# One order of a scheduled single-core kernel against another: W1 behind the inverse shuffles, k and v ahead of the filter, a last row stored in two parts

## Chip, cores and metric

The kernel runs on one core of a Trainium2 chip. The metric is the device time of one execution in microseconds (us). TensorE is called PE below, VectorE DVE, ScalarE ACT, GpSimdE POOL and SyncE SP.

## What is computed

The input x has 2048 positions and 448 channels. A long-convolution mixer comes first, then a perceptron over the positions (it multiplies along the 2048 positions, not along the channels). Cut to what matters:

```python
k_shift = sum(k_pad[:, t:t+S, :] * shift_k[:, ks-1-t] for t in range(4))   # short filter, 4 taps
kv = k_shift * v
y  = irfft(rfft(kv, padded to 2S) * rfft(ssm_k, padded to 2S))[:S]         # long convolution
h  = x + layernorm(x) * (y + kv * ssm_D)
n  = layernorm(layernorm(h))                                              # the outer and the block's own
u  = gelu(einsum("bsd,sf->bdf", n, w1) + b1)                              # w1: 2048 x 1792
h2 = h + transpose(einsum("bdf,fs->bds", u, w2) + b2)                     # w2: 1792 x 2048
```

All tensors are bfloat16. The Fourier transforms are done as matmuls with tables of sines and cosines that the kernel makes itself.

## The kernel before

Position s = 16 q + r lies in partition q, row r. So the tensors k, v and x have 16 rows of 448 channels in each of 128 partitions. The steps:

- **tables** (`emit_tables`): POOL and DVE make integer phases, ACT turns them into sines (`E`, in two halves; the second call is for the small tables `FW`, `MA`, `MB`, `MN`). A call of gelu on one column (L851) stands at the end. The functions of ACT need tables of their own; a change from Sin to gelu and back loads tables.
- **loads** (`emit_loads`), all on SP's queue: the long filter `KN` in four chunks of 112 channels, then the taps, k (`KH`) and v (`V`) in four groups of rows each, then D, b1, b2.
- **kT**: the filter is transposed on PE (L989) and copied to SBUF (`evac`, L712 on ACT and L715 on DVE). **kv**: k is transposed (L934), the short filter is done as matmuls with diagonal matrices (L953, 112 of them), and DVE multiplies with v (L959).
- **k1** and **u1** (`emit_stage1`): first stage of the transform of the filter and of kv, 128 matmuls each (L1009), copied to SBUF (L1019; L1017 adds D) and shuffled across partitions by DMAs from POOL and SP (L1025).
- **k2** and **u2** (`emit_stage2`): second stage, 64 matmuls each (L1044), copied with a scale for k (L713 on ACT, L716 on DVE) or without (L712, L715).
- **i1** (`emit_products_i1`): 16 products of the two transforms on DVE (L1077), first inverse stage on PE (L1089), copies, and the inverse shuffle by DMAs (L1113, the last ones L1102).
- **ct**: 32 transposes of `E` (L1058), whose result the next step needs. **q**: statistics of x on DVE and POOL (L1145, L1147, L1150, L1153).
- **i2** (`emit_i2`): second inverse stage (L1180, two matmuls per row), gate (L1187 ACT, L1189 DVE), combination with x (L1194) and both normalisations, which give `Q` (L1235).
- **mlp** (`emit_mlp`): first layer in 14 blocks of 128 columns over 16 rows, 112 matmuls with the first half of W1 (L1280) and 112 with the second (L1290), gelu on ACT (L1270), second layer with 14 matmuls per row (L1300), sum on DVE (L1304), stores from SP (L1308, L1311).

Matmuls whose result nobody reads (L979 "dummy", L1123 "warm") fill waits of PE.

The order on each engine is not that of the code. Every operation is recorded with what it reads and writes, and a list scheduler (`_Sched`) puts it on its engine: among the operations that are ready by its estimates, it takes the one with the smallest number in `WHEN`, a table with a rank per step. A fixed choice of ACT or DVE for the copies is in `WHERE`. Each engine then runs its own list strictly in that order and waits on semaphores. So a change of any estimate, rank or dependency can reorder all engines.

The weights come by SP's queue: the first two of four pieces of W1's first half (`W1A`) behind the u shuffles, the rest, the second half (`W1B`) and W2 behind the last inverse shuffle:

```python
op(WQ, lambda e, W, rs=rs: e.dma_start(W1A[:, rs, :], w1d[:, rs, 0:896]),
   w=[(o_W1A + 4 * h * 1792, 4 * 1792)], dmab=128 * 4 * 1792,
   after=shuf["u"] if h < 2 else [shuf["zpool"]])
```

Of the kernel before, what the change touches and what calls it, by code (L numbers as in the profile page):

```python
# [12 lines left out]
    "dummy": (104,),  # L13
    "tables": (10, 52, 67, 51, 209, 91, 219, 174,),
    "loads": (12, 63, 112, 113, 178, 199, 198, 217, 170, 184, 169, 207, 237, 226, 100,),
    "kv": (129, 6, 83, 4, 3, 157, 151, 194, 204, 85, 176, 65, 230, 9, 76, 163, 185,),
    "kT": (36, 46, 0, 53, 202, 195, 92, 71,),
    "k1": (14, 19, 30, 105, 94, 96, 116, 143, 108, 153, 127, 171, 167, 188, 190, 228,),
    "k2": (29, 28, 5, 11, 16, 27, 54, 88, 81, 57, 109, 138, 168, 172, 187, 192,),
    "u1": (8, 13, 34, 189, 24, 146, 149, 220, 175, 208, 215, 236, 48, 201, 213, 218,),  # L20
    "xload": (196, 135, 18, 31,),
    "ct": (239,),
    "bias": (43,),
    "q": (145, 130, 245, 253, 249, 242, 216, 251, 117,),
    "u2": (90, 25, 1, 26, 103, 107, 101, 99, 40, 102, 79, 15, 156, 134, 211, 214,),
    "i1": (123, 17, 106, 110, 7, 72, 55, 74, 89, 59, 177, 154, 73, 181, 222, 234,),
    "w1a": (66, 69, 98, 212,),
    "w1b": (97,),
    "warm": (224, 197, 200, 45, 39, 38, 42, 41, 162, 240, 238, 233, 227, 225, 193, 186, 124, 122, 161, 160, 158, 152,
        23, 78, 221, 56, 191, 144, 121, 95, 77, 210, 166, 86,),  # L30
    "i2": (141, 22, 35, 64, 87, 155, 147, 114, 126, 241, 75, 111, 115, 247, 203, 61, 229, 140, 179, 60, 142, 119, 137,
        139, 120, 136, 148, 128, 33, 93, 32,),
    "w2": (254,),
    "mlp": (159, 131, 248, 252, 250, 246, 244, 125, 132, 133, 37, 164, 58, 47, 50, 62, 182, 49, 118, 2, 165, 68, 44,
        150, 232, 205, 20, 231, 183, 180, 235, 173, 21, 80, 84, 206, 223, 82, 70, 243,),
}
WHERE = {
    "kv": "faffaaad",
    "kT": "ffaaafdf",
    "k1": "ffffaaadfddf",  # L40
    "k2": "fdffaddaffadffda",
    "u1": "ffafaadddddfdfad",
    "ct": "faaa",
    "bias": "a",
    "u2": "fdaafffaaaaddaaa",
    "i1": "aaffadafafaaaaaa",
    "i2": "faffdafaadaadddf",
# [518 lines left out]
def _build(nc, A_q, A_k, A_v, A_shift_k, A_ssm_k, A_ssm_D, B_w1, B_b1, B_w2, B_b2, out):  # L566
# [54 lines left out]
    with ctx:  # L621
# [65 lines left out]
        def Pb(b, i=0):  # L687
            return PS[:, b.slots[i], 0:D]
# [32 lines left out]
        def emit_tables():  # L721
# [85 lines left out]
            for h in range(2):  # L807
                sch.t0 = T_TH if h else -40.0
                o_ph = (o_pi, o_TK)[h]
                ph = view(o_ph, [64, 2, 16], i32)  # L810
                op("dve", lambda e, W, h=h, ph=ph: e.tensor_tensor(
                    out=ph[:, :, 1].rearrange("p (r x) f -> p r x f", x=8),
                    in0=frow.rearrange("p (x f) -> p x f", x=8).unsqueeze(1).broadcast_to([128, 8, 8, 16]),
                    in1=srow[:, 8 * h:8 * h + 8].unsqueeze(2).unsqueeze(3).broadcast_to([128, 8, 8, 16]), op=ALU.mult),
                   r=[(o_fr, 512), (o_s, 64)], w=[(o_ph, 8192)], n=HALF, kind="1x")
                op("dve", lambda e, W, ph=ph: e.tensor_scalar(
                    out=ph[:, :, 0], in0=ph[:, :, 1], scalar1=2048, scalar2=None, op0=ALU.add),
                   r=[(o_ph, 8192)], w=[(o_ph, 8192)], n=HALF, est=1020.0)
                phf = view(o_ph, [2 * HALF], i32)
                op("dve", lambda e, W, phf=phf: e.tensor_scalar(  # L820
                    out=phf, in0=phf, scalar1=8191, scalar2=None, op0=ALU.bitwise_and),
                   r=[(o_ph, 8192)], w=[(o_ph, 8192)], n=2 * HALF)
                op("act", lambda e, W, h=h, phf=phf: e.activation(
                    out=E[:, 16 * h:16 * h + 16, :].rearrange("p a f -> p (a f)"), in_=phf,
# [20 lines left out]
            for k, (dst, i) in enumerate(((FW, 0), (MA, 1), (MB, 1))):  # L845
# [5 lines left out]
            op("act", lambda e, W: e.activation(out=JK[:, 0:1], in_=bias[:, 1:2], func=ACT.Gelu_apprx_tanh),  # L851
               r=[(o_b + 4, 4), (o_sv, 4 * NB)], w=[(o_JK, 4)], est=1500.0)
# [7 lines left out]
        def emit_loads():  # L860
            Dq = "sp"
            for i, c in enumerate((3, 0, 1, 2)):
                sch.t0 = -20.0 + i
                op(Dq, lambda e, W, c=c: e.dma_start(KN[0:112, c, :], A_ssm_k[112 * c:112 * c + 112, :]),
                   w=[(o_KN + 4096 * c, 4096)], dmab=112 * 4096)
# [3 lines left out]
            for i, (src, c) in enumerate((("k", 3), ("k", 0), ("v", 0), ("k", 1), ("v", 1), ("k", 2), ("v", 2), ("v", 3))):  # L869
                sch.t0 = -14.0 + 0.5 * i  # L870
                if src == "k":
                    op(Dq, lambda e, W, c=c: e.dma_start(KH[:, 4 * c:4 * c + 4, :], k2d[:, 4 * c:4 * c + 4, :]),
                       w=[(o_KH + 4 * c * DB, 4 * DB)], dmab=128 * 4 * DB)
                else:
                    op(Dq, lambda e, W, c=c: e.dma_start(V[:, 4 * c:4 * c + 4, :], v2d[:, 4 * c:4 * c + 4, :]),
                       w=[(o_V + 4 * c * DB, 4 * DB)], dmab=128 * 4 * DB)
# [38 lines left out]
        def emit_kv():  # L915
# [3 lines left out]
            for i in range(2):  # L919
# [5 lines left out]
               r=[(o_ID, 256), (o_wsc, 64)], w=[(o_DG, 3584)], n=1792, kind="1x")  # L925
# [55 lines left out]

        def emit_kT():
            for i, c in enumerate((3, 0, 1, 2)):
                cw = 112
                for g in range(2):
                    sch.t0 = T_KT + 1.0 * (2 * i + g)
                    b = _Buf(psum)
                    for rr in range(8):
                        k = op("pe", lambda e, W, b=b, rr=rr, r=8 * g + rr, c=c, cw=cw: e.transpose(  # L989
                            out=Pbf(b, 0)[:, rr * cw:rr * cw + cw], in_=KN[0:cw, c, r:S:R], identity=ID[0:cw, 0:cw]),  # L990
                            r=[(o_KN + 4096 * c, 4096), (o_ID, 256)], bw=[b], kind="tr")
                    evac(lambda g=g, c=c, cw=cw: KT[:, 8 * g:8 * g + 8, 112 * c:112 * c + cw],
# [367 lines left out]
```

## Time and profile before

| what | value |
|---|---|
| median of 3 runs | 184.91 us (184.1 to 185.66) |
| the profiled execution | 185.73 us |
| its span | 183.5 us |
| PE busy | 172.5 us, 94% of the span |
| DVE busy | 108.1 us, 59% |
| ACT busy | 92.8 us, 51% |
| DMA read and written in HBM | 22.05 and 1.84 MB |

The span runs from the first to the last event that the profiler saw; the execution is 2.2 us longer. The page's second part divides the span into 40 slices of 4.6 us and gives the busy tenths of each engine. In the timelines a line has the start, the length, the engine, the source line, the operation with its shapes, how many instructions were merged, and in brackets how long the engine had stood idle and what ended that. The granted clock of PE was 1.0 throughout.

### The profile page before, as it was taken

How to read it: one execution, taken by the hardware profiler on the slowest of the kernel's cores; microseconds unless marked ns; L12 is line 12 of the kernel's file. 1: busy time of each engine (PE TensorE's matmuls, PEld its weight loads, DVE VectorE, ACT ScalarE, POOL GpSimd, SP SyncE). 2: the span in 40 equal slices, each digit the busy share in tenths (PEclk: the TensorE clock that was granted, in tenths of full speed). 3: DMA queues.
4: the chain of work that ended last, by engine and by line, in shares of the span. 5: the costliest groups of instructions: out<-in, count | busy, mean ns of one | idle time of the engine just before them, and what ended most of it. 6: DMA issues, size and time to landing. Idle time of an engine off the chain costs nothing.

```text
span 183.5 us, 3395 instructions
## 1 busy us (share of the span) xinstructions
PE 172.5 (94%) x1331; PEld 98.0 (53%) x1331; DVE 108.1 (59%) x180; ACT 92.8 (51%) x131; POOL 61.4 (33%) x155
## 2 busy tenths in 40 slices
PE   6989999999688898997999899999999999999996
PEld 2777645434233333463545355556556667777773
DVE  7978995897889999996989961000000008222221
ACT  3789877387879998966787473222102020000000
POOL 8053138299310509686788870000000000000000
DMA  6999028579849955777999999300000002011122
GB/s 176 265 377 384 12 100 326 180 261 330 303 138 379 393 207 150 221 206 237 396 405 406 424 416 425 129 0 0 0 4 0 0 0 75 4 50 50 54 96 75
DMA packets 15203, 35.11 MB, mean 191 GB/s; under 512 B 3580, under 2 KB 9244, under 8 KB 15188
## 3 DMA queue, kind: packets, MB, share of 16 engines
q1 hardware_dynamic: 12068, 28.09, 42.1%
q0 software_dynamic: 3072, 6.80, 11.4%
q8 instruction: 10, 0.16, 0.3%
q10 hardware_dynamic: 48, 0.03, 0.1%
q14 instruction: 5, 0.04, 0.1%
HBM read 22.05 MB, written 1.84 MB: 130 GB/s over the span
## 4 chain that ended last, share of the span: by engine, by line
PE 53%; DMA 14%; DVE 14%; ACT 9%; POOL 4%; SPq 3%; issue 3%; DVEq 0%; POOLq 0%
PE ps L1300 23%; PE ps L1290 12%; DMA arena<-arena 8%; PE ps L1280 6%; DMA arena<-in_A_v_dram 6%; ACT arena L712 6%; PE ps L953 4%; DVE arena L1194 3%; PE ps L1089 3%; DVE arena L1019 2%; PE ps L1009 2%; DVE arena L1077 2%; DVE arena L1145 2%; DVE arena L1235 2%; ACT arena L1019 1%
## 5 line engine op out<-in xcount | busy, mean ns | idle before, releaser
L1304 DVE SCALAR_TENSOR_TENSOR arena<-ps,arena 128x448 bf16<-128x448 f32 x16 | 10.9, 684 | 59.4 <-PE ps L1300 59.1
L1300 PE MATMUL ps<-arena 128*128 128x448 bf16 x224 | 43.9, 353 | 0.0
L1300 PEld LDWEIGHTS ps<-arena 128*128 128x128 bf16 x224 | 31.9, 144 | 11.0 <-ACT arena L1270 1.4
L1270 ACT ACTIVATE arena<-ps,arena 128x448 bf16<-128x448 f32 x14 | 8.5, 633 | 32.0 <-PE ps L1290 24.8
L1280 PE MATMUL ps<-arena 128*128 128x448 bf16 x112 | 24.2, 353 | 0.4 <-DVE arena L1235 0.4
L712 ACT CAST arena<-ps 128x896 bf16<-128x896 f32 (+1 forms) x29 | 23.4, 959 | 1.2 <-PE ps L1044 0.7
L1290 PE MATMUL ps<-arena 128*128 128x448 bf16 x112 | 23.3, 352 | 0.0
L1025 POOL DMA_DIRECT2D arena<-arena x32 | 17.6, 554 | 15.2 <-ACT arena L1019 9.3
L1019 ACT CAST arena<-ps 128x896 bf16<-128x896 f32 x17 | 14.7, 910 | 7.1 <-PE ps L1009 7.0
L1044 PE MATMUL ps<-arena 128*64 128x448 bf16 x128 | 14.9, 359 | 2.5 <-DMA arena<-arena 1.2
L712 ACT COPY arena<-ps 128x896 bf16<-128x896 bf16 (+2 forms) x14 | 13.2, 981 | 6.7 <-PE ps L989 3.5
L1280 PEld LDWEIGHTS ps<-arena 128*128 128x128 bf16 x112 | 10.8, 98 | 10.9 <-DVE arena L1235 1.3
L1077 DVE TENSOR_TENSOR arena<-arena 128x1792 bf16<-128x1792 bf16 x16 | 16.5, 1082 | 0.1
L1009 PE MATMUL ps<-arena 128*32 128x448 bf16 x256 | 15.2, 356 | 1.1 <-ACT arena L1019 0.5
L1290 PEld LDWEIGHTS ps<-arena 128*128 128x128 bf16 x112 | 10.9, 98 | 9.9 <-ACT arena L1270 0.2
L1089 PE MATMUL ps<-arena 64*128 64x448 bf16 x128 | 13.9, 352 | 1.7 <-ACT arena L712 1.4
L1113 POOL DMA_DIRECT2D arena<-arena x14 | 8.3, 596 | 16.7 <-ACT arena L712 16.5
L953 PE MATMUL ps<-arena 112*128 112x224 bf16 (+3 forms) x112 | 13.4, 273 | 0.0
L1019 DVE CAST arena<-ps 128x896 bf16<-128x896 f32 x11 | 11.5, 1084 | 0.8 <-PE ps L1009 0.6
L1044 PEld LDWEIGHTS ps<-arena 128*64 128x64 f16 x128 | 5.8, 108 | 11.2 <-ACT arena L712 3.6
L1194 DVE SCALAR_TENSOR_TENSOR arena<-arena 128x448 f32<-128x448 bf16 x16 | 10.6, 674 | 1.8 <-ACT arena L1187 1.7
L953 PEld LDWEIGHTS ps<-arena 112*128 112x128 bf16 x112 | 9.2, 98 | 4.2 <-issue 0.7
(90 smaller groups left out, 207.8 us busy)
## 6 DMA issues: line engine op xcount, KB each, us to landing
arena<-in_B_w_dram SPq DMA_DIRECT2D x8, 896.0 KB, 9.1
arena<-in_B_w_dram SPq DMA_DIRECT2D x2, 2048.0 KB, 16.4
arena<-arena SPq DMA_DIRECT2D x16, 224.0 KB, 4.0
arena<-arena POOLq DMA_DIRECT2D x32, 112.0 KB, 4.0
arena<-in_B_w_dram SPq DMA_DIRECT2D x2, 1536.0 KB, 20.4
arena<-arena POOLq DMA_DIRECT2D x14, 196.0 KB, 5.5
arena<-in_A_ssm_k_dram SPq DMA_DIRECT2D x4, 448.0 KB, 5.2
arena<-in_A_k_dram SPq DMA_DIRECT2D x4, 448.0 KB, 8.5
```

The costliest lines, as they stand in the source:

```text
L712: return e.copy(out=dst(), in_=src())
L953: op("pe", lambda e, W, b=b, i=i, cc=cc, dl=dl, i0=i0, i1=i1, rs=rs, sh=sh: e.matmul(Pb(b, i)[:, 112 * i0:112 * i1 + 112], KX[cc][0:112, i ...
L1009: op("pe", lambda e, W, b=b, r=r, q=q, x=x, c0=c0: e.matmul(PS[32 * q:32 * q + 32, b.slots[x], 0:D], E[:, 2 * r + x, c0:c0 + 32], src[:, r ...
L1019: return e.copy(out=dst, in_=Ppair(b)) if W == "act" else e.tensor_copy(out=dst, in_=Ppair(b))
L1025: shuf[tag].append(op(q_, lambda e, W, g=g, i=i, a=a, nu=nu, jh=jh: e.dma_start(T[a + i:a + i + 4 * nu - 3:4].rearrange("p (j k) c d -> p ...
L1044: op("pe", lambda e, W, b=bs[h], h=h, j=j, c=c, par=par: e.matmul(PS[64 * par:64 * par + 64, b.slots[c], 0:D], FW[:, 64 * c:64 * c + 64], ...
L1077: op("dve", lambda e, W, m=m, i=i: e.tensor_tensor(out=MR(m.slots[0]).rearrange("p (x y) d -> p x y d", x=2), in0=TU[:, i].unsqueeze(2).br ...
L1089: k = op("pe", lambda e, W, b=bs[h], m=ms[h], par=par, t=t, tab=tab, xy=xy, P=P: e.matmul(Pb(b, par), tab[P, :], MR(m.slots[0])[P, xy, :], ...
L1194: return e.scalar_tensor_tensor(out=A, in0=X[:, r, :], scalar=qs[:, r, 0:1], in1=A, op0=ALU.subtract, op1=ALU.mult, **({} if acc is None e ...
L1280: op("pe", lambda e, W, r=r, fc=fc, b=bs[fc]: e.matmul(Pb(b), W1A[:, r, 128 * fc:128 * fc + 128], Q[:, r, :], start=(r == 0), stop=(r == R ...
L1290: op("pe", lambda e, W, r=r, fc=fc, b=b: e.matmul(Pb(b), W1B[:, r, 128 * (fc - n0):128 * (fc - n0) + 128], Q[:, r, :], start=(r == 0), sto ...
L1300: op("pe", lambda e, W, r=r, fc=fc, b=b: e.matmul(Pb(b), W2[fc // 7][:, fc % 7, r:S:R], G[:, fc, :], start=(fc == 0), stop=(fc == NFC - 1) ...
```

## The change

It changes these parts:

- The tables of ranks (`WHEN`) and engines (`WHERE`) are new throughout.
- The long filter is loaded and transposed in chunks of 128, 128, 128 and 64 channels instead of four of 112. By the new ranks SP issues the first two groups of k ahead of it, and its last chunk behind all of k and v.
- The phases of `E` are kept as two contiguous blocks instead of interleaved in groups of 16, and Sin reads them through a strided view.
- The gelu call L851 is removed; the table for gelu is loaded at the first gelu of the perceptron (as it is before, too, since Sin follows L851).
- All of W1 waits for the last inverse shuffle issued, and W1 and W2 are issued in order.
- The last row's second layer is done in columns 0 to 319 and 320 to 447, each with its own sum and store, the first store from ACT's queue.
- Some estimates of the scheduler are changed.

By the new order the cosine transposes (now L1059) stand among the first transposes of k and of the filter, x is loaded in one go, and the eight warm matmuls that stood behind the last L1300 stand before i2. Line numbers move by a few: L953 becomes L950, L1009 L1010, L1044 L1045, L1077 L1078, L1089 L1090, L1180 L1181, L1280 L1283, L1290 L1293, L1300 L1305.

```diff
-    "loads": (12, 63, 112, 113, 178, 199, 198, 217, 170, 184, 169, 207, 237, 226, 100,),
+    "loads": (116, 139, 130, 216, 156, 20, 180, 206, 169, 196, 34, 211, 162, 241, 249,),
...
-    "ct": (239,),
+    "ct": (33,),
...
-                ph = view(o_ph, [64, 2, 16], i32)
+                ph = view(o_ph, [2, 8, 128], i32)
...
-                    out=ph[:, :, 0], in0=ph[:, :, 1], scalar1=2048, scalar2=None, op0=ALU.add),
-                   r=[(o_ph, 8192)], w=[(o_ph, 8192)], n=HALF, est=1020.0)
+                    out=ph[:, 0], in0=ph[:, 1], scalar1=2048, scalar2=None, op0=ALU.add),
+                   r=[(o_ph + 4096, 4096)], w=[(o_ph, 4096)], n=HALF)
...
-                    out=E[:, 16 * h:16 * h + 16, :].rearrange("p a f -> p (a f)"), in_=phf,
+                    out=E[:, 16 * h:16 * h + 16, :].rearrange("p a (b c f) -> p a b c f", b=4, c=2).rearrange("p a b c f -> p (a b) c f"),
+                    in_=ph.rearrange("p c r (g f) -> p c (r g) f", f=16).rearrange("p c g f -> p g c f"),
...
-            op("act", lambda e, W: e.activation(out=JK[:, 0:1], in_=bias[:, 1:2], func=ACT.Gelu_apprx_tanh),
-               r=[(o_b + 4, 4), (o_sv, 4 * NB)], w=[(o_JK, 4)], est=1500.0)
...
-            for i, c in enumerate((3, 0, 1, 2)):
+            for i, c in enumerate((0, 1, 2, 3)):
...
-                op(Dq, lambda e, W, c=c: e.dma_start(KN[0:112, c, :], A_ssm_k[112 * c:112 * c + 112, :]),
+                op(Dq, lambda e, W, c=c: e.dma_start(KN[0:CW[c], c, :], A_ssm_k[128 * c:128 * c + CW[c], :]),
...
+        CW = (128, 128, 128, 64)
...
-                    op(WQ, lambda e, W, rs=rs: e.dma_start(W1A[:, rs, :], w1d[:, rs, 0:896]),
+                    wl[0] = op(WQ, lambda e, W, rs=rs: e.dma_start(W1A[:, rs, :], w1d[:, rs, 0:896]),
                        w=[(o_W1A + 4 * h * 1792, 4 * 1792)], dmab=128 * 4 * 1792,
-                       after=shuf["u"] if h < 2 else [shuf["zpool"]])
+                       after=[shuf["zpool"]], safter=(wl[0],) if h else ())
...
+                for d0, d1 in ((0, D),) if r < R - 1 else ((0, 320), (320, D)):
...
+                    if r == R - 1:
+                        op("sp" if d0 else "act", lambda e, W, r=r, d0=d0, d1=d1: e.dma_start(o2d[:, r:r + 1, d0:d1], X[:, r:r + 1, d0:d1]),
+                           r=[(o_X + r * DB + 2 * d0, 2 * (d1 - d0))], dmab=128 * 2 * (d1 - d0), rate=400.0)
```

## The prediction

> **What bounds the kernel now.** I read the page first, then the chain of waits, then the engine timelines around each joint of that chain. The page shows which engine could be short where:
>
> ```profile
> PE   6989999999688898997999899999999999999996
> DVE  7978995897889999996989961000000008222221
> ACT  3789877387879998966787473222102020000000
> DMA  6999028579849955777999999300000002011122
> ```
>
> A slice is 4.6 us. TensorE (PE) reads 9 nearly everywhere, but not for one reason: until about 50 us DVE and ACT are below full beside it, from 55 to 77 us DVE is full as well, and from slice 23 on PE is alone. So three stages have three different limits, and I take them in turn.
>
> The chain of waits seems to say that the front waits for v:
>
> ```profile
> 6.41 11.67 DMA arena<-in_A_v_dram
> ...
> 18.17 1.10 DVE arena L959
> ...
> 19.32 0.56 PE ps L1009 x8
> ```
>
> and here is TensorE over the same time:
>
> ```profile
> 13.86 1.69 PE L934 MATMUL ps<-arena 128*112 128x128 bf16 x24
> 15.40 0.36 PE L953 MATMUL ps<-arena 112*128 112x448 bf16 x1
> ...
> 18.13 0.94 PE L1009 MATMUL ps<-arena 128*32 128x448 bf16 x16
> 19.32 0.56 PE L1009 MATMUL ps<-arena 128*32 128x448 bf16 x8 [0.24 <-DVE arena L959]
> ...
> 48.11 0.56 PE L1009 MATMUL ps<-arena 128*32 128x448 bf16 x8
> 49.84 1.71 PE L1044 MATMUL ps<-arena 128*64 128x448 bf16 x16 [1.17 <-DMA arena<-arena]
> ```
>
> Behind the 11.67 us load stands an idle time of 0.24 us. The rest of the load lies beside TensorE work. From the first filter matmul (15.40) to the last stage-1 matmul (48.11+0.56) there are 33.3 us with about 1.1 us of waits: **the front is bound by the amount of TensorE work**.
>
> Then DVE:
>
> ```profile
> 55.36 4.21 DVE L1077 TENSOR_TENSOR arena<-arena 128x1792 bf16<-128x1792 bf16 x4
> ...
> 74.84 2.08 DVE L1077 TENSOR_TENSOR arena<-arena 128x1792 bf16<-128x1792 bf16 x2
> ```
>
> From 54.35 to 76.92 it has no gap longer than 0.1 us: **the middle is bound by DVE**, 16 products and the copies between them. Last comes the tail. i2 starts at 84.93, when the inverse shuffle has landed, and the final L1300 ends at 180.65. These 95.7 us hold 32 i2, 448 MLP and 17 warm matmuls at 0.189 us (start to start), 94.0 us, so 1.7 us are waits. The end is this:
>
> ```profile
> 180.69 0.68 DVE L1304 SCALAR_TENSOR_TENSOR arena<-ps,arena 128x448 bf16<-128x448 f32 x1 [1.97 <-PE ps L1300]
> 181.40 0.33 SPq L1311 DMA_DIRECT2D out_dram<-arena  x1
> ```
>
> DVE 0.68, issue 0.33, landing 1.7 us after the issue began. The eight warm matmuls after 180.65 lie beside these.
>
> **Part by part, in order of time.**
>
> *k and v ahead of the filter, cosine transposes early.* In the changed program's order 142 transposes stand between the first nine dummies and the first filter matmul: 64 of k, 46 of the filter and all 32 of the cosine table (L1059). Before it is 113, with the cosine ones at 75 to 81 us, where 21 of 32 lay under the inverse shuffle. Both have nine more dummies there. The rows give 1.69/24 = 0.07 us a transpose and about 0.2 a dummy. k's first piece is issued where the filter's was (0.73) and I let it land alike, at 4.7. So: 4.92 (end of nine dummies) + 142 x 0.07 + 1.75 + 0.8 of waits (the 16 early cosine transposes wait for the first Sin, which I put at 7.7; before had 0.85) = 17.4. The first filter matmul comes at **17.4 instead of 15.4**. v is there by then. If k landed 1 us earlier nothing changes, since the dummies end at 4.92; if its second half (needed at row 26 of the order, about 13.8) were 1 us late, all of it is added.
>
> *New order up to the last stage-1 matmul.* The same 112 filter and 256 stage-1 matmuls follow; 18 filter transposes replace 16 of k; and 52 instead of 32 stage-2 matmuls of k stand ahead of the last stage-1 one. The rows give 0.107 to 0.124 us a stage-2 matmul: 20 x 0.11 = 2.2. The wait behind v goes (-0.24); the other 0.9 us of waits are kept, with bounds of 0.3 and 2.5, since 12 more copies fall into the last 10 us. 17.4 + 33.3 - 0.2 + 2.2 = 52.7 against 48.7: **+4.0 us**. One new wait is in there: b2 is now the last of the loads, and DVE's conversion of it stands ahead of the second filter product, with all stage-1 copies of DVE behind that. The D load took from 7.55 to 19.4, so b2 should land near 20, when DVE gets there (20.1): 0, and up to +1.
>
> *Tables.* The early gelu call (L851) goes, and with it a reload for Sin. ACT's rows are 1.28 (load), 0.20, 1.28 (load) from 17.47 to 20.28. The Trainium skill (ScalarE: Activation LUTs, What ACT_TABLE_LOAD costs) puts a switch at 1.28 us plus 1.38 of drain; two switches would give back 5.3 us. The trace shows the next instruction 0.01 us behind the load, so 2.8 us is what ACT gets back. Neither counts here: ACT idles 3.7 us at 31 to 35 anyway, and TensorE bounds this stretch. The gelu load at the first gelu stands in both orders (1.28 us at 108.5, TensorE busy beside it). The contiguous phase layout: the add took 1.32 beside GpSimd's work and 0.68 alone; taken as 0, bounds -0.6 and +0.3 (Sin now reads pieces of 16).
>
> *Middle.* Before, the last stage-1 copy ended at 49.89 and DVE's last product at 76.92, 27.0 later. After it DVE now has 3 + 4 copies instead of 3 + 5, so 1.0 less: 26.0. The product cannot start until all u shuffles have landed (5.5 us after that copy before) and now three copies stand ahead of it, so I take nothing more off. 49.9 + 4.0 + 26.0 = 79.9: **+3.0**. From the last product to the last copy it took 2.67 with a cosine copy of 1.07 in the way; without it 2.1: -0.5. On GpSimd's queue the three last shuffles now stand ahead of the first small statistics operation (0.24): -0.25. i2 starts at **+2.25**. The 30 warm matmuls there, 5.7 us, are covered by the 6.8 us of shuffle.
>
> *W1 behind the inverse shuffles.* SP issues all eight pieces from the landing on (before at 82.92, now 85.3). 0.92 MB at the 410 GB/s of 85 to 115 us is 2.24 each: first half of W1 at about 89.5, 91.8, 94, 96.3. Its first matmul comes 32 slots after i2 starts, at 93.4, and takes the next piece (four rows of seven matmuls) every 6 to 7 us. Hidden by about 4 us. W2 lands by 123, first used near 134. Queued behind these on SP are only stores, from 154 on. Cost 0.
>
> *i2 and MLP.* 18 warm matmuls before the last MLP ones instead of 17 (+0.2), DVE has one statistics operation and one gate fewer: 0 in all.
>
> *Last row in two parts.* 14 x 448 columns (2.65) become 14 x 320 and 14 x 128: 14 x 0.135 + 14 x 0.07 (the transposes' row) = 2.9, +0.25. The 320-part is stored from ACT's queue, empty since its last gelu; on DVE it lies beside the last seven small matmuls; the 128-part takes 0.34 and starts 0.11 behind them: done at 0.45 instead of 0.72. A rule speaks against: below 512 B a transfer is a read-modify-write (the Trainium skill, DMA: Bandwidth & Descriptors, Specifications), and this store writes 256 B a row. The rows: 112 KB land in 1.7, 224 KB in 1.9, so 0.2 per 112 KB and 1.5 fixed; 32 KB give 1.56 by the rows, 1.62 if the transfer counts twice. By either it lands no later than before. Part: +0.25 - 0.27 - 0.1 = **-0.1**, bounds -0.4 and +0.3.
>
> Sum: +2.25 + 0 + 0 - 0.1 = **+2.1**. The profiled execution took 185.73 (span 183.5), so 187.8. It lies 0.8 over the median of the runs shown, 184.91; on that scale 187.0. About 1% is what a measurement of this kernel can tell from no change.
>
> **Rivals.**
>
> *Front not held by the amount of work (faster).* If the 32 cosine transposes fit into holes that the trace of before shows as busy, and copies that v and the table loads held back flow earlier, the last stage-1 matmul comes near 48.7 again. Then the fewer copies show undiminished: -1.0 - 0.5 - 0.25 - 0.1, and 0.5 of i2's waits: 182.6. For it: the chain goes through v; ACT gets 2.8 us. Against: 0.24 us of idle behind v. Chance 0.27.
>
> *A wash.* Half of the front's loss comes back as fewer waits in the middle, TensorE having 20 stage-2 matmuls less to do there: +0.5, 185.4. Chance 0.23.
>
> *Weights late (slower still).* W1's first half arrives behind the normalised rows. It decides from 4 us of delay on; 3 us more is 190. Against: that margin. Chance 0.1.
>
> My forecast has 0.4. Faster by over 1%: 0.27; within: 0.23; slower: 0.5. The range, 182.2 to 190.2, reaches into the first rival since it holds more than 2 in 10; the likeliest case's own range is 185.4 to 189.
>
> **What would show it.** Right: first L950 near 17.4, last L1010 near 53, last product near 80, i2 near 87.2, and no wait for W1. Wrong: a last L1010 before 50 (the front was not work-bound), a product stretch much under 26 us, or PE waiting for a weight DMA after 90.

## The result, and the profile after

The changed kernel took **183.02 us** (median of 6 runs, 182.18 to 183.56) against 184.72 of the kernel before, run beside it (6 runs, 184.1 to 185.93): ratio **0.9884, 95% interval 0.9852 to 0.9915**. It is faster by 1.2%, where slower by 2.1 us was forecast. The profiled execution took 182.68 us, with a span of 180.7.

The page of the kernel after, busy tenths per slice (a slice is now 4.5 us):

```profile
PE   6999999999889999898999999999999999999994
DVE  7998676769889999998998565000000143322331
ACT  3897375788989999924878235441201200000000
DMA  5997008685884847774999999980000002002122
```

From slice 9 to slice 16 (41 to 77 us) DVE and ACT now read 8 or 9 together; before, ACT read 7 in two of the slices ahead of 55 us. Some copies that before does in the middle, after does in the front. The share of the engines in the chain that ended last, first before, then after:

```profile
PE 53%; DMA 14%; DVE 14%; ACT 9%; POOL 4%; SPq 3%; issue 3%; DVEq 0%; POOLq 0%
```

```profile
PE 78%; ACT 15%; DMA 2%; POOL 1%; issue 1%; DVE 1%; DVEq 0%
```

v (11.67 us in the chain before) is gone from it, and so are the products. What is left is PE, and ACT's copies. TensorE in the front of after (start, length, engine, line, shapes, instructions, idle time before them):

```profile
4.71 2.70 PE L931 MATMUL ps<-arena 128*112 128x128 bf16 x31
7.28 1.07 PE L1059 MATMUL ps<-arena 128*128 128x128 f16 x16
...
13.14 1.06 PE L1059 MATMUL ps<-arena 128*128 128x128 f16 x16
14.03 1.50 PE L931 MATMUL ps<-arena 128*112 128x128 bf16 x24
15.37 0.29 PE L989 MATMUL ps<-arena 128*128 128x128 bf16 x2
```

```profile
15.50 3.22 PE L950 MATMUL ps<-arena 112*128 112x448 bf16 x28
...
50.77 0.56 PE L1010 MATMUL ps<-arena 128*32 128x448 bf16 x8
51.26 0.95 PE L1045 MATMUL ps<-arena 128*64 128x448 bf16 x8
52.42 6.11 PE L1045 MATMUL ps<-arena 128*64 128x448 bf16 x48 [0.21 <-ACT arena L1020]
```

The first filter matmul is at 15.50, the last stage-1 one ends at 51.33. DVE from its last stage-1 copy (L1019 before, L1020 after) to its last product, first the start of it in before, then after:

```profile
48.80 1.09 DVE L1019 CAST arena<-ps 128x896 bf16<-128x896 f32 x1 [0.28 <-PE ps L1009]
50.83 3.09 DVE L716 TENSOR_SCALAR arena<-ps 128x896 bf16<-128x896 f32 x3 [0.94 <-PE ps L1044]
```

```profile
48.88 1.09 DVE L1020 CAST arena<-ps 128x896 bf16<-128x896 f32 x1
50.13 1.09 DVE L716 TENSOR_SCALAR arena<-ps 128x896 bf16<-128x896 f32 x1 [0.16 <-PE ps L1045]
51.90 2.25 DVE L716 TENSOR_SCALAR arena<-ps 128x896 bf16<-128x896 f32 x2 [0.68 <-PE ps L1045]
54.07 3.09 DVE L715 CAST arena<-ps 128x896 bf16<-128x896 f32 x3
57.07 11.45 DVE L1078 TENSOR_TENSOR arena<-arena 128x1792 bf16<-128x1792 bf16 x11
...
73.72 2.08 DVE L1078 TENSOR_TENSOR arena<-arena 128x1792 bf16<-128x1792 bf16 x2
```

The last stage-1 copy of all is DVE's own in before (it ends at 49.89); in after it is ACT's:

```profile
51.46 0.91 ACT L1020 CAST arena<-ps 128x896 bf16<-128x896 f32 x1 [0.42 <-PE ps L1010]
```

The end of after, on DVE and the two queues that store:

```profile
177.78 0.81 DVE L1308 SCALAR_TENSOR_TENSOR arena<-ps,arena 128x320 bf16<-128x320 f32 x2 [1.66 <-PE ps L1305]
178.36 0.38 ACTq L1313 DMA_DIRECT2D out_dram<-arena  x1
178.62 0.33 SPq L1313 DMA_DIRECT2D out_dram<-arena  x1
```

Cut at the joints that the prediction used (us; "four" is the mean of four profiles with before's order on PE: before and the runs e1, e2 and e16 below; in the last two rows it is the mean of before and e1 alone, since e2 and e16 change these two stretches):

| stretch | forecast of the change | before | four | after | after minus before | minus four |
|---|---|---|---|---|---|---|
| start to first filter matmul | +2.0 | 15.40 | 15.07 | 15.50 | +0.1 | +0.4 |
| to last stage-1 matmul | +2.0 | 33.27 | 33.12 | 35.83 | +2.6 | +2.7 |
| to last product | -1.0 | 28.25 | 28.20 | 24.47 | -3.8 | -3.7 |
| to i2 | -0.75 | 8.01 | 7.78 | 7.49 | -0.5 | -0.3 |
| to last matmul of L1300 / L1305 | +0.2 | 95.72 | 95.70 | 94.89 | -0.8 | -0.8 |
| to the end of the span | -0.4 | 2.85 | 2.86 | 2.52 | -0.3 | -0.3 |

The column "minus before" adds up to -2.8, more than the 2.1 us that the runs give (0.0116 x 184.7), because the profiled execution of before was a long one, as the prediction said; the column "minus four" adds up to -2.0. The front, up to the last stage-1 matmul, lost about 3 us where 4 were foreseen; the stretch from there to the last product gave back nearly four, where one was foreseen.

### The profile page after: what moved, and what is told of

Read it like the earlier page. It is cut to its first block, busy times and chain, and to the rows that moved or that the text cites. A ratio compares the mean times of both kernels' runs of the same rounds, so it can differ in the third digit from the quotient of the medians.

```text
span 180.7 us, 3417 instructions
## 1 busy us (share of the span) xinstructions
PE 172.7 (96%) x1345; PEld 99.4 (55%) x1345; DVE 105.4 (58%) x181; ACT 89.8 (50%) x128; POOL 62.0 (34%) x155
## 4 chain that ended last, share of the span: by engine, by line
PE 78%; ACT 15%; DMA 2%; POOL 1%; issue 1%; DVE 1%; DVEq 0%
PE ps L1305 23%; PE ps L1283 12%; PE ps L1293 12%; ACT arena L712 8%; PE ps L950 7%; PE ps L1010 5%; ACT arena L1020 5%; PE ps L1181 4%; PE ps L976 3%; ACT arena L713 3%; PE ps L1045 3%; DMA arena<-arena 2%; PE ps L931 2%; PE ps L989 2%; PE ps L1090 2%; PE ps L1124 2%
## 5 line engine op out<-in xcount | busy, mean ns | idle before, releaser
L1308 DVE SCALAR_TENSOR_TENSOR arena<-ps,arena 128x448 bf16<-128x448 f32 (+2 forms) x17 | 11.1, 656 | 55.3 <-PE ps L1305 55.3
L1305 PE MATMUL ps<-arena 128*128 128x448 bf16 (+2 forms) x238 | 43.0, 342 | 0.0
L1305 PEld LDWEIGHTS ps<-arena 128*128 128x128 bf16 x238 | 33.0, 144 | 9.9 <-ACT arena L1273 0.5
L712 ACT CAST arena<-ps 128x896 bf16<-128x896 f32 x28 | 23.2, 986 | 0.5 <-DVE arena L1148 0.2
L1283 PE MATMUL ps<-arena 128*128 128x448 bf16 x112 | 23.5, 353 | 0.0
L1293 PE MATMUL ps<-arena 128*128 128x448 bf16 x112 | 22.0, 352 | 0.0
L1020 ACT CAST arena<-ps 128x896 bf16<-128x896 f32 x22 | 18.8, 912 | 6.4 <-PE ps L1010 6.0
L1045 PE MATMUL ps<-arena 128*64 128x448 bf16 x128 | 16.0, 361 | 1.1 <-ACT arena L1020 0.7
L1078 DVE TENSOR_TENSOR arena<-arena 128x1792 bf16<-128x1792 bf16 x16 | 16.6, 1084 | 0.2
L1283 PEld LDWEIGHTS ps<-arena 128*128 128x128 bf16 x112 | 10.9, 98 | 10.5 <-DVE arena L1236 0.6
L1293 PEld LDWEIGHTS ps<-arena 128*128 128x128 bf16 x112 | 11.0, 98 | 10.2
L1090 PE MATMUL ps<-arena 64*128 64x448 bf16 x128 | 13.9, 352 | 1.8 <-ACT arena L712 1.2
L1010 PE MATMUL ps<-arena 128*32 128x448 bf16 x256 | 14.6, 355 | 0.5 <-ACT arena L713 0.3
L950 PE MATMUL ps<-arena 112*128 112x224 bf16 (+3 forms) x112 | 13.4, 273 | 0.0
L1211 ACT ACTIVATE arena<-arena 128x448 bf16<-128x448 f32 x14 | 8.1, 576 | 7.7 <-DVE arena L1195 7.5
L1188 ACT ACTIVATE arena<-ps,arena 128x448 f32<-128x448 f32 x12 | 8.1, 722 | 7.5 <-PE ps L1181 7.5
L950 PEld LDWEIGHTS ps<-arena 112*128 112x128 bf16 x112 | 9.2, 98 | 4.4 <-DVE arena L1020 0.8
L1045 PEld LDWEIGHTS ps<-arena 128*64 128x64 f16 x128 | 5.2, 108 | 11.4 <-ACT arena L712 3.7
```

The costliest lines, as they stand in the source:

```text
L712: return e.copy(out=dst(), in_=src())
L950: op("pe", lambda e, W, b=b, i=i, cc=cc, dl=dl, i0=i0, i1=i1, rs=rs, sh=sh: e.matmul(Pb(b, i)[:, 112 * i0:112 * i1 + 112], KX[cc][0:112, i ...
L1010: op("pe", lambda e, W, b=b, r=r, q=q, x=x, c0=c0: e.matmul(PS[32 * q:32 * q + 32, b.slots[x], 0:D], E[:, 2 * r + x, c0:c0 + 32], src[:, r ...
L1020: return e.copy(out=dst, in_=Ppair(b)) if W == "act" else e.tensor_copy(out=dst, in_=Ppair(b))
L1045: op("pe", lambda e, W, b=bs[h], h=h, j=j, c=c, par=par: e.matmul(PS[64 * par:64 * par + 64, b.slots[c], 0:D], FW[:, 64 * c:64 * c + 64], ...
L1078: op("dve", lambda e, W, m=m, i=i: e.tensor_tensor(out=MR(m.slots[0]).rearrange("p (x y) d -> p x y d", x=2), in0=TU[:, i].unsqueeze(2).br ...
```

## The experiments

The theory that the runs were to test (A in most expectations): front and middle trade against each other at about one to one, since copies of the second stage done in the front leave DVE and ACT in the middle, and the net gain comes from i2 and the tail. Rivals: the tables, the placement of W1, or the cosine transposes are the gain. All ratios are to the kernel before, with 95% intervals.

### Parts alone: tables, split, ranks, gelu

```diff
 e1_tables_only (on before, L851)
-    func=ACT.Gelu_apprx_tanh)
+    func=ACT.Sin)
 e2_split_only (on before): the last row's code of after
 e3_ranks_only (on before)
-WHEN, WHERE of before
+WHEN, WHERE of after
 e4_gelu_back (on after)
+    op("act", lambda e, W: e.activation(out=JK[:, 0:1], in_=bias[:, 1:2], func=ACT.Gelu_apprx_tanh), ..., est=1.0)
```

> The kernel before with the early call of gelu turned into a call of Sin: the same instructions in the same order on every engine, without the two table loads (2.56 us of ACT at 17.5 to 20.3 us). Theory A (the gain is the new order of the middle: the filter's second stage is done before kv's first stage ends): ratio 0.998 to 1.001, since ACT idles 3.7 us some 11 us later. Rival B (what holds the front is ACT and the loads, so the table loads are the gain): the last stage-1 copy ends 1.5 to 2.5 us earlier than 49.9, ratio 0.987 to 0.992.

> The kernel before with its last row done and stored in two parts, nothing else. From the two traces, end of the last matmul to end of span fell from 2.85 to about 2.45 us, and the last row costs about 0.25 us more of TensorE: Theory A: ratio 0.998 to 1.000 (-0.1 to -0.4 us). Rival C (the tail is the gain, the stages before it give nothing in the median): ratio 0.992 to 0.995.

> The kernel before with the new tables of ranks and engines and nothing else: chunks of 112, early gelu call, early W1, one last store stay. Theory A: the order carries the gain, ratio 0.985 to 0.992, last product 23 to 25 us behind the last stage-1 copy. Rivals B and C: the parts carry it, ratio 0.996 to 1.004.

> The changed kernel with the early gelu call put back behind the small tables' Sin: the same order on every engine, with a table load and a call (1.5 us) more on ACT at about 17.4 us, where ACT idles 1.5 us and then 1.6 us (and a load for gelu less at 108 us if it stays loaded). Theory A: ratio to before as the changed kernel's, 0.986 to 0.991. Rival B: 1.5 us slower, 0.994 to 0.998.

- **e1: 1.0002 (0.9978 to 1.0026).** Without the two table loads ACT is done earlier and then idles longer. ACT in e1:

```profile
16.67 0.21 ACT L851 ACTIVATE arena<-arena 128x1 bf16<-128x1 f32 x1
16.77 2.00 ACT L823 ACTIVATE arena<-arena 128x2048 f16<-128x2048 int32 x1
22.19 1.01 ACT L712 COPY arena<-ps 112x1024 bf16<-112x1024 bf16 x1 [3.42 <-PE ps L934]
```

  The idle of 3.42 us was 0.62 in before. **e4: 0.9905 (0.9873 to 0.9936)**, like after, says the same from the other side: no gain of the table loads shows, within about 0.25% (e1).
- **e2: 0.9999 (0.9973 to 1.0025).** In the trace i2 to the end of the span took 98.26 instead of 98.57 us; the runs can't tell 0.3 us.
- **e3: 1.0708 (1.0662 to 1.0754).** The expectation failed. Last stage-1 matmul at 56.06, and 7.6 us more from there to i2 than in after (39.6 against 32.0). With the chunks of 112 channels and before's estimates the new ranks give another order, with waits for DMA (the longest, 2.09 us, directly behind the last stage-1 group) and a mean granted clock of 0.983. Ranks and code belong together; "the order" can't be moved to other code as a table.

### Order changed through ranks or dependencies

```diff
 e5_ct_late (on after)
-    r=[(o_E + 2048 * h + 256 * i, 256), (o_IH, 256)], bw=[b], kind="tr")
+    r=[(o_E + 2048 * h + 256 * i, 256), (o_IH, 256)], bw=[b], kind="tr", after=i1_last[-1:])       # and ct recorded behind i1
 e6_no_dummy (on after)
-    N_WZ, N_WI, N_W0, N_WK, N_WJ = 34, 6, 9, 3, 8
+    N_WZ, N_WI, N_W0, N_WK, N_WJ = 34, 6, 9, 0, 8
 e7_k1u1_before (on after)
-    "k1", "u1": ranks of after
+    "k1", "u1": ranks of before
 e8_late_stat (on after)
-    "q": (159, 69, 115, 108, 117, 102, 175, 176, 193,),
+    "q": (159, 69, 115, 108, 117, 102, 175, 255, 193,),
 e9_k2_held (on after; k2 recorded behind u1)
+    after=s1[-1:] if scale and jj >= 4 else ()      # on the k2 matmuls; s1: last stage-1 matmul
 e10_before_k2_ahead (on before)
-    "k2": (29, 28, 5, 11, 16, 27, 54, 88, 81, 57, 109, 138, 168, 172, 187, 192,),
+    "k2": (29, 28, 5, 11, 16, 27, 54, 88, 81, 57, 57, 57, 57, 57, 57, 57,),
 e11_half_ct_late (on after): e5's edit for the second half of ct alone, N_WZ 34 -> 26
```

> The kernel after, but the 32 cosine transposes are released only by the last first-inverse-stage matmul, as they were placed before, under the inverse shuffle. Theory A (the front is bound by the amount of PE work, each early cosine transpose is paid there): first filter matmul and last stage-1 matmul 1.7 to 1.8 us earlier than in after (13.7 and 49.5), i2 start 1.0 to 1.8 us earlier if the transposes' two copies stay under the shuffle, so ratio to before 0.979 to 0.984. Theory B (the front waits for data and copies, the early transposes lie in its holes): last stage-1 matmul within 0.4 us of 51.3, i2 start the same or up to 0.5 later, ratio 0.988 to 0.993.

> The kernel after without the nine unread matmuls that stand among the filter's transposes (1.75 us of PE by the prediction). Theory A (the first filter matmul comes when PE has worked through its list): first filter matmul at 13.8 instead of 15.5, last stage-1 matmul 1.7 earlier, ratio to before near 0.979. Theory B (PE would wait for k, the filter's chunks or the copies in the same place): first filter matmul within 0.4 us of 15.5, the 1.7 us appear as waits, ratio 0.986 to 0.992.

> The kernel after with the ranks of the first transform stage of filter and kv taken from before: 24 instead of 52 second-stage matmuls of k stand ahead of the last stage-1 matmul, the other 28 and their 7 copies behind it. Theory A (in the middle DVE is the bound, so a copy of k2 that is done in the front beside PE is free and in the middle is paid at about 0.9 us; PE's 28 x 0.11 in the front is what it costs): last stage-1 matmul 3 us earlier (48.3), time from the last stage-1 copy to i2 3 to 4 us longer than after's 30.9, i2 start 0 to 1 us later, ratio to before 0.988 to 0.995. Theory B (the middle became shorter for other reasons: cosine transposes, x, shuffle order): the middle stays at 31 to 32 us, i2 starts 2 to 3 us earlier, ratio 0.972 to 0.978.

> The kernel after with the small statistics of one group of rows (number 6) released last, into i2, as before had them; PE's order is unchanged but for two unread matmuls. Theory A (i2 to the end became 1.2 us shorter because no row waits for a late statistic): i2 start within 0.2 us of 83.3, waits of 0.2 to 0.6 us for DVE appear in PE or DVE around 93 to 105 us, span 0.4 to 1.0 longer than after, ratio to before 0.991 to 0.996. Theory B (that stretch is shorter for other reasons, such as first-layer matmuls standing between the rows): no wait, span within 0.3 of after, ratio 0.987 to 0.990.

> The kernel after, but the last eight of sixteen groups of second-stage matmuls of k are released only by the last stage-1 matmul of kv: by its order 12 of the 52 that stood ahead of that matmul (three groups with their copies) come behind it, and the front is otherwise the same. Theory A (the middle became shorter because copies of k2 were done in the front beside PE; in the middle each is paid by DVE or ACT): last stage-1 matmul about 1.3 us earlier (12 x 0.107), time from the last stage-1 copy to i2 start 1.3 to 2.7 us longer than the 30.9 of after, i2 start from 0 to 1.4 later, ratio to before 0.988 to 0.996. Theory B (the middle is shorter because of the cosine copies, x and the order of the shuffles): that time stays within 0.5 of 30.9, i2 starts about 1.3 earlier, ratio 0.980 to 0.984.

> The kernel before, with nothing changed but the ranks of the last six groups of k's second stage, so that they come as early as the tenth: the order is the same up to the last 8 stage-1 matmuls of kv; then more second-stage matmuls stand ahead of these, fewer behind them, and the cosine transposes move ahead of the products. Theory A (copies of k2 done in the front are free, in the middle they are paid): last stage-1 matmul 3 to 5 us later than 48.7, time from the last stage-1 copy to i2 at 29 to 31 us instead of 34.3 to 35.0, i2 start between 1.5 earlier and 1.5 later, ratio 0.990 to 1.008. Theory B (the middle keeps its 34 us): i2 3 to 5 us later, ratio 1.016 to 1.027.

> The kernel after, but only the second half of the cosine transposes (the 16 behind the second Sin) is released by the last first-inverse-stage matmul, and there are eight unread matmuls fewer under the inverse shuffle and in i2, so that the order of i2 stays near that of after. Theory A (of the 32 early transposes only the 16 behind the last group of k stand on the path, 0.95 us): last stage-1 matmul 0.9 to 1.1 us earlier than 51.3, i2 start 0.9 to 1.2 earlier, the rest as in after, ratio to before 0.981 to 0.985: faster than both. Theory B (i2 loses it again by its new order, as in the run with all 32 late): ratio 0.988 or more.

- **e6: 0.9879 (0.9851 to 0.9907).** Theory B. The first filter matmul came at 15.69, not at 13.8; the time of the nine unread matmuls turned into waits. TensorE in e6:

```profile
12.06 0.62 PE L931 MATMUL ps<-arena 128*112 128x128 bf16 x8 [0.52 <-DMA arena<-in_A_k_dram]
12.88 1.55 PE L931 MATMUL ps<-arena 128*112 128x128 bf16 x24 [0.20 <-ACT arena L712]
14.79 1.07 PE L1059 MATMUL ps<-arena 128*128 128x128 f16 x16 [0.36 <-ACT arena L821]
```

  So around 12 us k's landing sets the pace, then the copies and the second Sin; the dummies stood in a wait.
- **e5: 1.0278 (1.0251 to 1.0304).** The last stage-1 matmul came at 50.27, 1.06 us earlier (between the theories; e11, which moves the second half alone, keeps 0.8 of it, so the first half looks nearly free), and i2 at 82.11, 1.18 earlier. But i2 took another order and lost 9 us; more on it in the last section.
- **e11: 0.9937 (0.9914 to 0.996).** The front kept 0.8 us, i2's new order lost it: i2 to the last matmul took 96.35 instead of 94.89.
- **e7: 1.1149 (1.11 to 1.1198)** and **e9: 1.0347 (1.0294 to 1.0399)**, **e10: 1.0597 (1.0559 to 1.0636)** failed both of their theories. In e9 the scheduler put 44 matmuls of stage 2 between the last two stage-1 groups, and the last group waited for copies on ACT.

  That group ended at 57.11 instead of 51.33, and the shuffle behind it was left with little beside it (PE waited 2.74 us for it). e10 went the same way (59.44). These three are inconclusive on what they asked, since the order changed too much.
- **e8: 0.9877 (0.9845 to 0.9909).** Theory B: with the last aggregates moved into i2 (96.58 and 98.71 us) after loses nothing (i2 to the last matmul 94.89, as in after).

### Named instructions moved in a held order

The runs before this mixed their question with a new order of everything behind. The next ones take the order of each engine as a list after scheduling, move only the named instructions in it, and allot the buffers anew (lines are shifted by some 50 in their profiles).

```diff
 e13_ct_half_moved (on after)
+    place(pe, second 16 of ct, behind last i1); their 2 copies to act, behind its last shuffle issue
+    drop(the last 12 of the 34 warm matmuls that follow i1)
 e14_k2_back (on after)
+    place(pe, the last 12 k2 ahead of the last stage-1 group, behind it); place(act, 1 copy, behind its last u1 copy)
 e15_k2_ahead (on after)
+    place(pe, the 12 k2 behind the last stage-1 group, ahead of it); place(act, 2 copies, ahead of its last u1 copy)
 e16_before_stats_early (on before)
+    place(dve and pool, the q operations that stand within i2, ahead of i2)
 e17_ct_half_b2_late = e13
+    place(dve, L909, behind the last product)
 e18_w1_two_early (on after)
+    first two W1A: wait for the u shuffles instead; place(sp, them, behind the last u shuffle)
 e12_no_split (on after): the last row's code of before; same order otherwise
```

> The kernel after with the last row's second layer in one piece and one store from SP, as before; the order is otherwise the same. Theory A (the split is worth the 0.35 us by which the tail behind the last matmul became shorter, less the time by which PE works longer): span 0.1 to 0.4 longer than after, ratio to before 0.989 to 0.992. Theory B (the split costs on PE what it saves behind it): span within 0.1, ratio 0.986 to 0.989.

> The kernel after with the order of every engine held as a list, in which the 16 cosine transposes behind the second Sin are moved behind the last first-inverse-stage matmul, their two copies behind ACT's last shuffle issues, and 12 unread matmuls (8 there, 4 in the second inverse stage) are left out. Nothing else moves. Theory A (16 of the 32 early transposes are paid in the front, all of the rest is as before): first filter matmul at 14.6, last stage-1 matmul at 50.4 to 50.6, i2 start 0.8 to 1.0 earlier, i2 to the end as in after, ratio to before 0.981 to 0.986. Theory B (the granted time comes back as waits for v, copies or shuffles): ratio 0.987 to 0.991.

> The kernel after with the order of every engine held as a list, in which the last 12 second-stage matmuls of k that stand ahead of the last stage-1 group (three groups) are moved behind it, and the one copy of ACT that stood ahead of the last stage-1 copy too; DVE's two follow in their places. Theory A (DVE and ACT together are the bound of the middle; 40 copies behind the last stage-1 copy took 27.0 us in before and 34 took 23.4 in after, 0.6 us each): last stage-1 matmul 1.3 to 1.6 us earlier, the time from the last stage-1 copy to the last product 1.5 to 2.0 longer than 23.4, i2 start from 0 to 0.6 later, ratio to before 0.988 to 0.993. Theory B (the copies fit into the 4.7 us in which the products wait for the u shuffles): that time up to 0.6 longer, i2 about 1 earlier, ratio 0.980 to 0.985.

> The same the other way: the last 12 second-stage matmuls of k and their copies are moved from behind the last stage-1 group to ahead of it, so that all 64 stand in the front. Theory A (0.6 us a copy in the middle against 0.43 to 0.6 a group in the front): last stage-1 matmul 1.3 to 1.8 us later, time from the last stage-1 copy to the last product 1.5 to 2.0 shorter, i2 start within 0.5 of 83.3, ratio 0.985 to 0.991. Theory B (the hole behind the last stage-1 copy hides these copies, so moving them ahead only costs): i2 1 to 1.5 us later, ratio 0.993 to 0.998.

> The kernel before with the order of every engine held as a list, in which the last statistic of x (three small operations on DVE and two on GpSimd) is moved from within the second inverse stage to ahead of it, where after has it. PE's order is the same. Theory A (this late statistic is what makes PE wait 0.9 us between 93 and 105 us): the waits of 0.36, 0.33 and 0.25 us for DVE go, i2 start to end 0.5 to 0.9 shorter than 98.5, ratio 0.995 to 0.998. Theory B (the waits come from the order of the rows on PE, with too few first-layer matmuls between them): waits stay, ratio 0.999 to 1.003.

> As the run with half of the cosine transposes moved (held order, 16 of them and their two copies behind the last first-inverse-stage matmul, 12 unread matmuls left out), and DVE's conversion of b2 is moved behind the last product, so that nothing in the front waits for b2. Theory A (b2, loaded last, became the limit of the front once the transposes were gone): no idle of DVE for b2 ahead of the products with v, first filter matmul at 14.6, last stage-1 matmul at 50.3 to 50.6, i2 start near 82.3, ratio to before 0.980 to 0.985, faster than both kernels. Theory B (v, D or the shuffles hold the front there as well): last stage-1 matmul at 51 or later, ratio 0.986 or more.

> The kernel after with the order of every engine held as a list, in which only the first two pieces of W1's first half wait for the u shuffles as in before, and stand on SP directly behind these, ahead of x. Theory A (where W1 waits is worth nothing: no matmul waits for a weight, and the pieces flow in a stretch with spare transfer time): every stage within 0.4 us of after, ratio to before 0.986 to 0.992. Theory B (1.8 MB of weights beside the shuffles and x delay the statistics of x or the inverse shuffles, and this is the part of the gain behind the last product): i2 starts 0.4 to 1.0 later, ratio 0.991 to 0.996.

**e14: 0.9878 (0.9848 to 0.9907), e15: 0.9911 (0.9881 to 0.994).** Both are like after up to about 47.5 us. Counted from the start of the last run of 24 stage-1 matmuls that the three share (47.81 in after, 47.48 in e14, 47.47 in e15):

| | to last stage-1 matmul | to last product |
|---|---|---|
| e14, three groups of k2 back | 2.01 | 28.08 |
| after | 3.52 | 27.99 |
| e15, three groups ahead | 5.45 | 28.78 |

Three groups moved back bring TensorE's last stage-1 matmul 1.5 us forward, and the last product comes no earlier: the ratio and the start of i2 (83.66) are nearer theory A of e14. But its price of 0.6 us a copy did not come out: from the last stage-1 copy to the last product it took 24.6 us, 1.2 more than in after, where 1.5 to 2.0 was said. (The 40 and 34 copies of that expectation are 38 and 34 when both are counted up to the last product.) In e15, three groups ahead, the last stage-1 matmul comes 1.9 us later and the product 0.8: between its two theories. DVE in e15 then waits for TensorE behind these copies:

```profile
53.98 1.09 DVE L767 CAST arena<-ps 128x896 bf16<-128x896 f32 x1 [0.68 <-PE ps L1097]
55.47 2.09 DVE L767 CAST arena<-ps 128x896 bf16<-128x896 f32 x2 [0.39 <-PE ps L1097]
57.47 5.44 DVE L1130 TENSOR_TENSOR arena<-arena 128x1792 bf16<-128x1792 bf16 x5
```

The two runs show more than they were made for. DVE's list is the same in both, and its own last stage-1 copy ended at 49.70 us in both. TensorE's last stage-1 matmul ended at 49.49 in e14 and at 52.92 in e15, 3.4 us apart; the last product ended at 75.56 and 76.25, only 0.7 apart. In these orders the product follows DVE's list, not the end of TensorE's stage 1.

**e16: 0.9955 (0.9926 to 0.9984).** The late statistic of before costs it about 0.4%. TensorE in i2, first before, then e16 (L1180 is L1230 there):

```profile
93.45 1.12 PE L1280 MATMUL ps<-arena 128*128 128x448 bf16 x5 [0.36 <-DVE arena L1235]
...
102.09 0.55 PE L1180 MATMUL ps<-arena 128*128 128x448 bf16 x2 [0.33 <-DVE arena L1189]
...
104.24 0.54 PE L1180 MATMUL ps<-arena 128*128 128x448 bf16 x2 [0.25 <-DVE arena L1235]
```

```profile
93.30 1.12 PE L1330 MATMUL ps<-arena 128*128 128x448 bf16 x5 [0.36 <-DVE arena L1285]
...
101.49 0.55 PE L1230 MATMUL ps<-arena 128*128 128x448 bf16 x2
...
103.60 0.54 PE L1230 MATMUL ps<-arena 128*128 128x448 bf16 x2 [0.22 <-DVE arena L1285]
```

The middle wait is gone, the other two stay, and i2 to the last matmul takes 95.24 instead of 95.72: 0.48 of the 0.83 us. So theory A holds for one of the three waits. After has none of them; that the other 0.35 comes from its order of rows is only argued.

**e12: 0.9919 (0.9896 to 0.9943).** PE ended 0.11 us earlier relative to i2 (94.78), the tail, from there to the end of the span, took 2.91 instead of 2.52. The split is worth about 0.3 us in the trace (theory A); the times don't contradict it.

**e18: 0.9916 (0.988 to 0.9952).** Product end, 75.94, and i2 start, 83.69, are within 0.4 us of after, at the edge of theory A. Where W1 waits is worth between nothing and about half a microsecond; the interval doesn't settle it.

**e13: 0.987 (0.9837 to 0.9902), e17: 0.9851 (0.9815 to 0.9887).** Half of the cosine transposes out of the front brought the first filter matmul to 14.64 and 14.61, 0.9 us earlier, and both times it was given back before the end of the front (theory B of both). In e13 DVE stood idle for b2, the last of the loads, with the products of v behind it; PE waited 0.37 and 0.53 us there, and 0.83 for k's shuffle later. In e17 the wait for b2 is gone, and PE, 0.9 us ahead until 44.4, waits for k's shuffle. DVE of e13, then PE of e17:

```profile
19.91 0.18 DVE L963 CAST arena<-arena 128x16 f32<-128x16 bf16 x1 [2.46 <-DMA arena<-in_B_b_dram]
```

```profile
45.21 0.57 PE L1101 MATMUL ps<-arena 128*64 128x448 bf16 x4 [0.80 <-DMA arena<-arena]
```

The last stage-1 matmul ended at 52.55 in e13, at 51.25 in e17 and at 51.33 in after. One profile fixes this joint no better than to some 0.7 us: e8 and e12 have after's order up to there, and ended it at 52.01 and 51.83. Neither version is shown to be faster than after: their intervals overlap with its own.

## Why the prediction was wrong, by its steps

- **The step that failed: where DVE's part of the middle begins.** The prediction let the last stage-1 copy move with TensorE's last stage-1 matmul (49.9 + 4.0) and put 26.0 us of DVE behind it, which gave 79.9. In before DVE copied the last stage-1 group itself, so its copy had to follow that matmul (49.89 behind 48.67). In after ACT copies it, and DVE's own last stage-1 copy ended at 49.97, 1.4 us ahead of TensorE's last stage-1 matmul (51.33). That is +0.1 against before's 49.89, not +4.0: 1.9 of the difference is the first filter matmul (below); the other 2.0 was booked for 20 more stage-2 matmuls of k in the front, but 12 of these and the last stage-1 group stand behind the matmuls that DVE's last stage-1 copy waits for.
- **DVE's list itself was right.** From its own last stage-1 copy to the last product DVE took 27.03 us before and 25.83 after. Forecast were 26.0, with 3 + 4 copies, and these are the copies that stand there. So the last product came at 75.80, 4.1 us earlier than forecast: 3.9 by the start and 0.2 by the length. Eleven profiles with the same seven copies (after, e4 to e6, e8, e11 to e14, e17, e18) all took 25.8 to 26.1; e15 took 26.6, since DVE waits longer for TensorE there. And e14 and e15 show that 3.4 us on TensorE's joint move the product by 0.7.
- **The same by the joints of the table.** From the last stage-1 copy of any engine to the last product it took 27.0 before and 23.4 after, the "product stretch much under 26 us". Up to the last product DVE has 6 copies there instead of 8 and 1.2 us less idle time; ACT has 28 instead of 30. ACT was as full as DVE, which the prediction did not say. Busy time in before and then in after (stretch, length, then busy time and instructions of PE, its loads, DVE, ACT, POOL; clock, DMA share, GB/s):

```profile
54.40:76.90 22.50, 19.93 (x190) 7.53 (x186) 22.41 (x26) 22.01 (x27) 9.24 (x14) 1.00 0.81 269
```

```profile
56.90:75.80 18.90, 17.04 (x154) 5.84 (x152) 18.70 (x22) 18.73 (x24) 7.01 (x12) 1.00 0.70 224
```

  The page that the prediction quoted showed it: ACT's row reads 9, 9, 9, 8, 9 from 55 to 78 us. The chain that ended last in after even goes through ACT's copies (ACT 15%, DVE 1%). Whether DVE alone or both bound the middle stays open: no run moved a copy from one to the other and nothing else.
- **First filter matmul: 15.50, not 17.4.** Two terms were mis-sized. From the start of the transposes at 4.71 to 15.50, less 1.70 us of dummies, 142 transposes took 9.1 us: 0.064 each instead of 0.07, which is 0.8 us. The wait of 0.8 for Sin wasn't there: Sin ended at 7.22 and the transposes started at 7.28. And the stretch was not a sum of work (e6): unread matmuls taken out turned into waits.
- **The rest of the front: +2.6 where +2.0 was said.** The 20 more k2 matmuls are there, and some waits for their copies (0.32, 0.25, 0.21). The end of the front, 51.33, was right by its direction: more work of PE, later end (52.7 forecast). That work alone bounds it is too strong: with the front 0.9 us ahead, TensorE waited for k's shuffle (e17). The bound on b2, 0 and up to +1, was apt: in after DVE stood idle 0.79 us for b2 and TensorE did not wait; e13, with a faster front, paid 0.9 us.
- **Tables 0: right** (e1, e4). The load for gelu, at 109.69, took 1.28 us, beside PE at work.
- **Behind the last product: -0.75 forecast, -0.5 measured**; -0.3 against the four profiles.
- **W1 behind the shuffles, 0: right within e18's interval.** SP issued at 83.21, no matmul waited for a weight.
- **i2 and the perceptron: 0 forecast, -0.8 measured.** The prediction counted warm matmuls and overlooked that 0.94 us of waits stood in before's i2; it named 1.7 us of waits there and didn't ask for their cause. e16 shows 0.48 of it.
- **Last row: -0.1 forecast, -0.3 measured.** PE lost 0.11, not 0.25. The 256 B rows landed no later: from the last issue to the end of the span 2.1 us, as with the whole row (181.40 to 183.5 before, 178.62 to 180.7 after).

The rival that came nearest in time (182.6) was near for another reason: it had the last stage-1 matmul stay near 48.7, and that came at 51.3. The sign given for a wrong forecast, a product stretch much under 26 us, is the one that appeared. What stays open: of the gain of 2.1 us the statistic (about 0.5, in before's order) and the split (0.3, in the trace) have runs of their own. The last product came 0.6 us earlier than in the mean of the four profiles of before's order. One DVE copy fewer behind DVE's own last stage-1 copy, the forecast -1.0, is the likely source, since it was no longer outweighed by a late start; that is read from the traces, and no run tested that copy alone. W1's place is worth between nothing and 0.5 us (e18).

## What to carry to other kernels

Where a stage is bound by one engine, count it from that engine's own last instruction of the stage before, and not from a joint of another engine: in the old order DVE's copy followed TensorE's last stage-1 matmul, in the new one it ended 1.4 us ahead of it, and a delay of TensorE was charged to DVE, which hardly felt it. Ask of work that is added in front of a joint which engine behind it really waits for that work. And read every engine's row in the stage: ACT was as full as DVE. Last, a wait that is taken away uncovers the next one: twice here (b2, then the shuffle of k) 0.9 us gained in the front came to nothing.

## What the runs showed of the hardware that was not expected

The granted clock fell without a long gap. In e5 the rows of i2 followed each other singly, each waiting 0.8 us for the gate of the last. The windows' columns are as above; after them TensorE:

```profile
100.00:105.00 5.00, 3.24 (x16) 1.11 (x13) 1.99 (x5) 1.52 (x4) 0.00 (x0) 1.00 1.05 415
105.00:110.00 5.00, 2.71 (x7) 0.68 (x8) 2.92 (x8) 3.87 (x10) 2.46 (x8) 0.51 1.02 421
110.00:115.00 5.00, 5.00 (x23) 2.26 (x22) 3.05 (x7) 1.19 (x4) 2.76 (x7) 0.80 1.02 420
```

```profile
102.95 0.55 PE L1181 MATMUL ps<-arena 128*128 128x448 bf16 x2 [0.82 <-ACT arena L1188]
104.28 0.55 PE L1181 MATMUL ps<-arena 128*128 128x448 bf16 x2 [0.78 <-DVE arena L1190]
105.65 0.93 PE L1181 MATMUL ps<-arena 128*128 128x448 bf16 x2 [0.82 <-ACT arena L1188]
```

Two matmuls that took 0.55 us take 0.93 at a clock of about 0.5, and in windows of 1 us the clock is back at 1.00 from 112 us on. All six runs of e5 show it in their mean clock, 0.982 or 0.991. The Trainium skill (TensorE: Matmul & The Clock Gate, Why this matters for your kernels) asks for no idle gap above about 3 us between bursts; here no single wait was longer than 0.82 us. In the 3 us ahead of the fall (102 to 105 us) TensorE was busy 1.24 us, about 40%. That the share of busy time, and not the length of one gap, brings the clock down is a reading of this one place; no run varied it. It may be a reason for unread matmuls in such places, though none shows it: where 4 of them were left out of i2 (e13, e17), i2 to the last matmul took under 0.1 us more.
